# A fourth gate/up group in the space of late h tiles, q k v loads ahead of all groups, w_down loads late, and a p*v sum by a copied bank

## The chip, the cores and the metric

The kernel runs on one core of one Trainium2 chip. The metric is device time in microseconds (us) of one execution; lower is better. Times of profiled executions come from one execution each, and the median stands over three timed runs without a profile.

## The reference

One transformer-like block over 2048 tokens of width 576, in bf16. A layer norm feeds an attention with 32 heads of 18 columns and a sliding window of 256 tokens, and a gated feed-forward network of inner width 4608. The two results are multiplied and added to the input.

```python
xn = layernorm(x)                                   # 2048 x 576
q, k, v = split(xn @ wqkv)                          # 32 heads of 18
scores = q @ k.T * 18 ** -0.5, kept where 0 <= i - j < 256
s = (softmax(scores) @ v) @ wo
h = sigmoid(xn @ w_gate) * (xn @ w_up)              # 2048 x 4608
g = silu(h @ w_down)
out = x + s * g
```

## The kernel before

The tokens are worked in four chunks of 512 columns (`CH`, four blocks of 128). A chunk c passes these stages:

- **Layer norm** (`build_ln`): statistics and mean on VectorE, the power for the reciprocal deviation on POOL (`rstd`), normalising on VectorE (`apply`, L424), a copy of the first 64 columns behind the last (`wrap`, L428, so that two halves of TensorE's rows see matching pieces). In chunk 0 the result is transposed by TensorE (L447) and copied by ScalarE; in the others by a transposing DMA into `xn`.
- **Projections** (`build_qkv`, `project`, L468): twelve projections of 18 matmuls each. In chunk 0 q and k of a block go into one buffer (`pk` or a spare part of `expr`), and one transposing DMA per block brings both into `qkp`.
- **Attention**: `build_unit` computes scores (L613) into PSUM banks 0 to 3, ScalarE takes exponentials (L631), VectorE multiplies masks (L649). `build_pv` multiplies with v for a pair of head groups (L683), again into banks 0 to 3, two banks per head group, because the two halves of TensorE's rows fill a bank each. VectorE then transposes both banks of a head group (L699, L701), adds them (L704), divides (L713, L717) and transposes back (L723, `after_pv`); DMAs gather the heads in `oT`.
- **Gate and up** (`build_ffn`, L830): 36 tiles of 128 inner columns, 18 matmuls each. A tile's gate and up sums take two of the PSUM banks 4 to 7; ScalarE takes tanh (L844), VectorE forms the product (L848) and writes the tile into `hT`. The weights come in 12 groups of 3 tiles through a ring of `RW` = 3 buffers (`wgs`), each group by four DMAs (`load9`).
- **Down** (`f2`, L954, last block L984): four blocks of 128 tokens, each with 9 w_down loads' worth of matmuls (`op_wd`); the 9 loads happen once, in chunk 0, and stay. **wo** (`build_wo`, L760) multiplies the attention's result for two pairs of blocks. `build_final` forms the output (L1015 to L1023).

Between these stages the order isn't written by hand. Every piece of work is an `Op` with an engine, an estimated duration, dependencies and a priority; `schedule` is a greedy planner that places, at each step, the operation that can start first by these estimates, plus 40 ns per point of priority (`PRIO_NS`), and so fixes the instruction order of each engine. Dependencies in `odeps` and `behind` only order; those in `deps` also become semaphore waits (`emit`). All DMAs are issued by one queue, SP's, in the planner's order, so that one that waits holds up all behind it.

The first chunk differs from the others in that nothing is loaded yet. `QKV_LOAD` and `W_PRIO` set the order of the weights: q, v, group 0, k, groups 1 and 2, the transposes of q and k (L216), then group 3 and so on as ring buffers come free. `build_late_weights` lets w_down's load q go when gate/up tile 3 q + 8 is done.

Of the kernel before, what the change touches and what calls it, by code (L numbers as in the profile page):

```python
# [8 lines left out]
D = 576  # L9
# [25 lines left out]
RW = 3  # L35
RT = 2
# [17 lines left out]
WX_FT = 7  # L54
QKV_FIRST = "q0 q1 v0 v1 q2 v2 k0 v3 k1 q3 k2 k3"
# [3 lines left out]
QKV_CHAIN = 0  # L59
# [4 lines left out]
F2B = ((0, 1), (2, 3), (6, 7), (4, 5))  # L64
# [15 lines left out]
LN_STEP = 1  # L80
XT_CUT = 4
SC_GATE = 0
QKT_BEHIND = {2: 0}
# [3 lines left out]
QKV_LOAD = (-8, -4, -6)  # L87
W_PRIO = (-5, 2, 3)
# [4 lines left out]
XT0_BYTES = 1.2  # L93
# [83 lines left out]
class Builder:  # L177
# [46 lines left out]
    def alloc_memory(self):  # L224
# [44 lines left out]
        self.pkf = self.pk.bitcast(f32)  # L269

# [4 lines left out]
    def build(self):  # L275
# [22 lines left out]
        for c in range(NCH):  # L298
# [14 lines left out]
            if c == 0:  # L313
                self.build_late_weights()
                for o in self.ops:
                    if o.name.startswith("wo:0:") and o.fence is None:
                        o.add_dep(self.op_wo)

    def build_init(self):
# [22 lines left out]
        self.op_pkz = [op("ACT", 1300 + 1500, lambda e: e.memzero(self.pk[:, :, :, :]), "pkz", prio=0)]  # L342
        self.op_pkz.append(op("ACT", 2500, lambda e: e.memzero(self.expr[:, 0:3, :, :]), "pkz2", prio=0))
# [29 lines left out]
    def build_late_weights(self):  # L373
# [12 lines left out]
        for q in range(NWD):  # L386
            self.op_wd[q].add_dep(self.op_f1[(0, 3 * q + 8)])
# [7 lines left out]
    def build_ln(self, c):  # L395
# [4 lines left out]
        for i in range(QPC):  # L400
            st = c * QPC + i
            if c == 0:
# [15 lines left out]
            ve = op("DVE", 100, lambda e, st=st: e.tensor_scalar(self.veps[:, st, :], self.mv[:, st, 1:2], EPS,  # L418
                                                                None, ALU.add), f"ve:{st}", deps=[ag], prio=pr)
# [8 lines left out]
            wr = op("DVE", 100, lambda e, sr=sr: e.tensor_copy(self.xnr[:, sr, D:DP], self.xnr[:, sr, 0:64]),  # L428
                    f"wrap:{st}", deps=[ap], prio=pr)
# [10 lines left out]
            for i0, i1, dep in ((0, XT_CUT, ap), (XT_CUT, NC, wr)):  # L440
# [9 lines left out]
                tr = self.pe(n * 58, f_tr, f"tr:{st}", deps=[dep, self.op_ident] + dxn, prio=pr, psum=[ps])  # L450
# [8 lines left out]
        self.all_xn = [o for l in self.op_xn for o in l]  # L459

# [29 lines left out]
    def build_qkv(self, c):  # L490
# [4 lines left out]
        for w in order.split():  # L495
            i, j = int(w[1]), "qkv".index(w[0])
            o = (self.build_v if j == 2 else self.build_qk)(c, i, j, old)
            if c > 0:
                o.odeps += ([prev] if prev and QKV_CHAIN else []) + (self.op_xn[QKV_GATE] if not prev else []) + ([self.f2_ops[QKV_F2]] if QKV_F2 else [])
                o.prio = QKV_PRIO  # L500
            prev = o

    def build_qk(self, c, i, j, old):
# [8 lines left out]
        o, ps = self.project(c, i, j, f"qk:{c}:{i}:{j}", dpk, self.op_pv[c - 1][NHG - 1] if c > 0 else None)  # L512

        def f_ev(e):
# [5 lines left out]
            if j == 0:  # L520
# [3 lines left out]
                     deps=[o, self.op_pkz] + [t for t in (self.op_on[c - 1] if c > 0 else [])], prio=1, psum=[ps])  # L524
        if c == 0:
            if j == 0:
# [4 lines left out]
                          prio=0, issue=XT0_ISSUE_NS, transpose=True)  # L531
# [123 lines left out]
    def build_pv(self, c, a):  # L655
# [38 lines left out]
        bufs = {a: (self.tf[:, :, :, :].rearrange("p a b d -> p (a b d)"), pkf[1]), a + 1: (pkf[0], pkf[1])}  # L694
        ads = []
        qk = self.op_q + self.op_k
        for hg in pair:
            tf, tg = bufs[hg]
            t1 = self.rd("DVE", dve_ns(CH), lambda e, tf=tf, hg=hg: e.transpose(tf, self.bank(ps2[hg][0])),  # L699
                         f"t1:{c}:{hg}", deps=[o, self.last_mul] + qk, prio=3, psum=ps2[hg][:1])  # L700
            t3 = self.rd("DVE", dve_ns(CH), lambda e, tg=tg, hg=hg: e.transpose(tg, self.bank(ps2[hg][1])),  # L701
                         f"t3:{c}:{hg}", deps=[o, self.last_mul] + qk + ads, prio=3, psum=ps2[hg][1:])
            tf, tg = (t.rearrange("p (g d) -> p g d", d=32)[:, :, 0:DH + 1] for t in (tf, tg))
            ads = [self.op("DVE", dve_ns(16 * (DH + 1)), lambda e, tf=tf, tg=tg: e.tensor_tensor(tf, tf, tg, ALU.add),  # L704
                           f"ad:{c}:{hg}", deps=[t1, t3], prio=3)]
            bufs[hg] = (tf, ads[0])
        for hg in pair:
            self.after_pv(c, hg, o, *bufs[hg])

# [35 lines left out]
    def build_wo(self, c):  # L745
# [3 lines left out]
        for pair in ((0, 2), (1, 3)):  # L749
# [3 lines left out]
            def f_wo(e, swap, ps2=ps2, pair=pair):  # L753
                for kt in range(NKT - swap):
                    for n, (n0, n1) in enumerate(((0, 512), (512, D))):
                        for hf in range(2):
                            w = hf ^ swap
                            r0 = 64 * hf
                            qi = pair[w]
                            r = e.matmul(self.bank(ps2[w], n1 - n0, n), self.oT[r0:r0 + 64, kt, qi * P:(qi + 1) * P],  # L760
                                         self.wo_sb[r0:r0 + 64, kt, n0:n1], start=(swap == 0 and kt == 0),
                                         stop=(swap == 1 and kt == NKT - 2), tile_position=(r0, 0))
                return r
            wa = self.pe(NKT * (mm_ns(512) + mm_ns(64)), lambda e, f=f_wo: f(e, 0), f"wo:{c}:{pair[0]}",
                         deps=self.op_oc[c][0] + self.op_oc[c][1] + self.op_wo + [d for _, ds in slots for d in ds],
                         prio=WO_PRIO, psum=ps2, mode="r64")
            wo = self.pe((NKT - 1) * (mm_ns(512) + mm_ns(64)), lambda e, f=f_wo: f(e, 1), f"wo:{c}:{pair[0]}s",
                         deps=[wa], prio=WO_PRIO, mode="r64")
            wo.fence = wa
            for ps in ps2:  # L770
                ps.users.append(wo)
            for qi, ps, (ss, _) in zip(pair, ps2, slots):
                def f_se(e, ps=ps, ss=ss):
                    b = ps.banks[0] * 512
                    return e.activation(self.sat[:, ss, :], self.ps[:, b:b + D], ACTF.Copy, scale=0.25)
# [17 lines left out]
    def build_ffn(self, c):  # L793
        pg = [Psum((6,), (7,), (5,), (4,)) for _ in range(NFT)]
        pu = [Psum((6,), (7,), (5,), (4,)) for _ in range(NFT)]
        slots, dmas = {}, {}
# [20 lines left out]
        for n0, n1 in zip(cuts, cuts[1:]):  # L817
            if n1 - n0 > RUN:
                cuts.append(n0 + (n1 - n0 + 1) // 2)
# [4 lines left out]
        def step(e, half, gu, ft, i, x):  # L824
            r0 = 64 * half
            f0 = ft % FG * P
            w = (self.wgs[r0:r0 + 64, slots[ft // FG], i, f0:f0 + P] if x is None
# [441 lines left out]
```

## Time and profile before

| | us |
|---|---|
| median of three timed runs (566.16 to 566.95) | 566.52 |
| profiled execution, device time | 568.96 |
| its span, first to last instruction | 566.8 |
| TensorE busy in it | 558.1 |
| VectorE / ScalarE / POOL busy | 308.5 / 275.0 / 28.3 |

| stretch of the profiled execution | us |
|---|---|
| warm matmuls, transposes and eight projections | 1.52 to 17.49 |
| gate/up and the last four projections until the first scores | 17.49 to 37.55 |
| first chunk's down matmuls begin | 108.5 |
| down matmuls of chunks 1, 2, 3 begin | 246.9, 385.0, 523.1 |
| end | 566.8 |

The granted TensorE clock is 0.999 in the mean. Busy times are those of one execution; a row of the timeline gives start, duration, engine, line of the kernel, output and inputs, the number of instructions that follow each other, and in brackets the idle time before the first and what ended it. "PE" is TensorE, "DVE" VectorE, "ACT" ScalarE, "SPq" the queue that issues DMAs.

### The profile page before, as it was taken

The numbers are of one execution on the slowest core, as the hardware profiler recorded it, in microseconds if no ns is written. First come the engines' busy times: TensorE is split into PE (matmuls) and PEld (weight loads), VectorE is DVE, ScalarE is ACT, GpSimd is POOL, SyncE is SP. The second block draws the span as 40 slices with busy tenths as digits, with TensorE's granted clock in tenths as the row PEclk, the third lists the DMA queues.
The fourth block names the chain that finished last, engine by engine and source line by source line (L and its number), as shares of the span: only waits on it lengthen the run. The fifth ranks groups of instructions, "written<-read, shape, count | busy, mean of one in ns | idle before, by whom it ended". The sixth has DMA issues, their size and how long they took to land.

```text
span 566.8 us, 17897 instructions
## 1 busy us (share of the span) xinstructions
PE 558.1 (98%) x7854; PEld 282.9 (50%) x7854; DVE 308.5 (54%) x664; ACT 275.0 (49%) x372; POOL 28.3 (5%) x55
## 2 busy tenths in 40 slices
PE   8999989999999999999999999999999999999997
PEld 5644434457544444455654444545665444444544
DVE  6137987831236895782204778767120686686213
ACT  7447656403246847721406676581230856856011
POOL 3000100010000000010000011001000000000100
PEclk9999999999999999999999999999999999999999
DMA  8999999538966666324894665614669455650001
GB/s 198 212 200 232 237 216 219 131 71 104 164 128 148 149 138 148 87 47 77 110 213 103 143 154 130 152 46 61 98 111 210 97 127 128 147 130 23 20 22 43
DMA packets 125898, 73.29 MB, mean 129 GB/s; under 512 B 54654, under 2 KB 125310, under 8 KB 125822
## 3 DMA queue, kind: packets, MB, share of 16 engines
q1 hardware_dynamic: 125822, 72.16, 62.8%
q8 instruction: 62, 1.02, 0.8%
q14 instruction: 14, 0.11, 0.1%
HBM read 55.48 MB, written 2.36 MB: 102 GB/s over the span
## 4 chain that ended last, share of the span: by engine, by line
PE 94%; SPq 2%; DMA 2%; issue 1%; DVE 0%; ACT 0%
PE ps L830 50%; PE ps L954 23%; PE ps L468 8%; PE ps L613 5%; PE ps L683 4%; PE ps L760 3%; SPq L217 2%; PE ps L984 2%; DMA wqkv_sb<-in_A_wqkv_dram 1%; DMA qkp<-expr 1%; ACT expr L631 0%; DVE hT L848 0%; DVE expr L649 0%; DVE thf L1017 0%; ACT thf L1015 0%
## 5 line engine op out<-in xcount | busy, mean ns | idle before, releaser
L830 PE MATMUL ps<-xn,wgs 64*128 64x512 bf16 x2576 | 296.5, 377 | 0.2 <-DVE hT L848 0.2
L830 PEld LDWEIGHTS ps<-xn,wgs 64*128 64x128 bf16 x2576 | 119.5, 94 | 142.3 <-issue 7.6
L631 ACT ACTIVATE expr<-ps 128x1024 bf16<-128x1024 f32 x152 | 147.2, 1022 | 25.3 <-PE ps L613 25.3
L954 PE MATMUL ps<-wd_sb,hT 128*128 128x512 bf16 (+1 forms) x1080 | 133.7, 286 | 0.0
L844 ACT ACTIVATE tring<-ps 128x512 bf16<-128x512 f32 x144 | 86.3, 600 | 86.4 <-PE ps L830 84.4
L848 DVE SCALAR_TENSOR_TENSOR hT<-tring,ps 128x512 bf16<-128x512 bf16 x144 | 98.0, 680 | 31.5 <-ACT tring L844 15.0
L954 PEld LDWEIGHTS ps<-wd_sb,hT 128*128 128x128 bf16 x1080 | 68.3, 98 | 64.9 <-issue 1.4
L649 DVE TENSOR_TENSOR expr<-expr,m 128x512 bf16<-128x512 bf16 (+2 forms) x152 | 58.4, 412 | 53.7 <-ACT expr L631 52.5
L1015 ACT ACTIVATE thf<-ps 128x576 bf16<-128x576 f32 (+2 forms) x17 | 10.6, 623 | 134.3 <-PE ps L954 127.1
L1017 DVE SCALAR_TENSOR_TENSOR thf<-thf,ps 128x576 bf16<-128x576 bf16 (+2 forms) x17 | 12.2, 719 | 107.6 <-ACT thf L1015 107.6
L468 PE MATMUL ps<-wqkv_sb,xn 64*128 64x288 bf16 x864 | 54.7, 283 | 0.8 <-DMA wqkv_sb<-in_A_wqkv_dram 0.8
L468 PEld LDWEIGHTS ps<-wqkv_sb,xn 64*128 64x128 bf16 x864 | 42.5, 94 | 11.9 <-issue 2.0
L613 PE MATMUL ps<-qkp 18*64 18x320 bf16 (+4 forms) x1472 | 32.4, 259 | 0.9 <-DMA qkp<-expr 0.9
L613 PEld LDWEIGHTS ps<-qkp 18*64 18x64 bf16 x1472 | 16.2, 103 | 33.4 <-ACT expr L631 14.0
L660 POOL COPY qkp<-qkp 128x256 bf16<-128x256 bf16 x24 | 9.6, 401 | 282.2 <-PE ps L613 282.2
L683 PE MATMUL ps<-expr,vau 64*32 64x320 bf16 (+5 forms) x1440 | 20.9, 253 | 2.1 <-issue 1.9
L683 PEld LDWEIGHTS ps<-expr,vau 64*32 64x32 bf16 x1440 | 18.0, 92 | 9.6 <-issue 6.4
L723 DVE STREAM_TRANSPOSE op__63<-pk 128x512 bf16<-128x512 bf16 x32 | 22.3, 697 | 0.2
L521 DVE CAST pk<-ps 128x576 bf16<-128x576 f32 x13 | 9.8, 754 | 21.5 <-PE ps L468 21.5
L701 DVE STREAM_TRANSPOSE pk<-ps 128x512 f32<-128x512 f32 x32 | 21.5, 671 | 0.0
L760 PE MATMUL ps<-wo_sb,oT 64*128 64x512 bf16 (+1 forms) x288 | 18.7, 283 | 0.1
L699 DVE STREAM_TRANSPOSE tf<-ps 128x512 f32<-128x512 f32 x16 | 11.5, 717 | 13.0 <-PE ps L683 12.9
(54 smaller groups left out, 201.1 us busy)
## 6 DMA issues: line engine op xcount, KB each, us to landing
wgs<-in_B_w_gate_dram SPq DMA_DIRECT2D x48, 240.0 KB, 3.8
wgs<-in_B_w_up_dram SPq DMA_DIRECT2D x48, 240.0 KB, 4.8
wgs<-in_B_w_up_dram SPq DMA_DIRECT2D x48, 192.0 KB, 4.1
wgs<-in_B_w_gate_dram SPq DMA_DIRECT2D x48, 192.0 KB, 4.5
wd_sb<-in_B_w_down_dram SPq DMA_DIRECT2D x9, 576.0 KB, 7.7
xf<-in_A_x_dram SPq DMA_DIRECT2D x18, 144.0 KB, 2.3
out_dram<-xf SPq DMA_DIRECT2D x15, 144.0 KB, 2.0
xr<-in_A_x_dram SPq DMA_DIRECT2D x14, 144.0 KB, 5.0
```

The costliest lines, as they stand in the source:

```text
L468: r = e.matmul(self.bank(ps, HV, hf), self.xn[r0:r0 + 64, k, i * P:(i + 1) * P], self.wqkv_sb[r0:r0 + 64, j, k, :], start=(k == 0), stop=( ...
L613: r = e.matmul(self.ps[64 * half:64 * half + 64, b:b + n * 64], self.qkp[r0:r0 + DH, hg, k0:k0 + 64], self.qkp[r0:r0 + DH, hg, q0 * 64:(q0 ...
L631: return e.activation(self.expr[:, es, 2 * pr:2 * pr + 2, :], src, ACTF.Exp, scale=SM_SCALE)
L649: return e.tensor_tensor(ap, ap, m, ALU.mult)
L683: r = e.matmul(self.ps[32 * j:32 * j + 32, b + q0 * 64:b + (q0 + n) * 64], vf[:, v0:v0 + 32], self.expr[p0:p0 + 64, es, j, pos * 64:(pos + ...
L701: t3 = self.rd("DVE", dve_ns(CH), lambda e, tg=tg, hg=hg: e.transpose(tg, self.bank(ps2[hg][1])), f"t3:{c}:{hg}", deps=[o, self.last_mul] ...
L723: t2 = self.op("DVE", dve_ns(CH), lambda e, on=on: e.transpose(self.op_[:, hg % NOT, :], on.rearrange("p g d -> p (g d)")), f"t2:{c}:{hg}" ...
L760: r = e.matmul(self.bank(ps2[w], n1 - n0, n), self.oT[r0:r0 + 64, kt, qi * P:(qi + 1) * P], self.wo_sb[r0:r0 + 64, kt, n0:n1], start=(swap ...
L830: return e.matmul(self.bank((pg, pu)[gu][ft]), w, self.xn[r0:r0 + 64, i, :], start=first, stop=last, tile_position=(r0, 0))
L844: return e.activation(self.tring[:, st_, :], self.bank(ps), ACTF.Tanh, scale=0.5)
L848: return e.scalar_tensor_tensor(self.hT[:, ft, :], self.tring[:, st_, :], 1.0, self.bank(ps), ALU.add, ALU.mult)
L954: r = e.matmul(self.ps[:, b + n0:b + n1], lhsT, self.wd_sb[:, q, fl, n0:n1], start=(ft == 0), stop=(ft == NFT - 1))
```

## The change

The change has several parts, nearly all in the first chunk.

- **Loads.** The k weights come ahead of all groups. Group 3 of chunk 0 gets a place of its own: `far`, the space of `hT`'s tiles 29 to 35, which the products fill near the chunk's end. Its four loads stand ahead of the q/k transposes. A gate/up operation waits for the one of a group's four loads that it reads, no longer for all four.
- **w_down.** Load q waits for gate/up tile 14, 18, 22, 28, 29, 30, 31, 32, 33 and not for 8, 11, ..., 32.
- **Layer norm.** The addition of epsilon and the wrap go from VectorE to POOL; the wrap is computed from x and no longer copied from the normalised tile. Tiles' priorities are further apart.
- **Clearing.** ScalarE clears two buffers of `pk` and three parts of `expr` one by one, the last behind the transposes.
- **p*v in chunk 0** (`pv_by_copy`): ScalarE copies one bank of a head group into SBUF, VectorE adds the other bank to it and transposes the sum once.
- **wo** is cut into four passes of 288 columns (two per bank half), not two passes of 512 and 64. In chunks 1 to 3 the order of projections is fixed, and wo stands after the fourth and the sixth of them.
- **Priorities** of tanh, product and p*v change, a run of 9 steps is cut 4 + 5 and not 5 + 4, the last down block's banks have two candidates, and down matmuls after the first block come after the chunk's last p*v.

What the planner makes of it on TensorE in chunk 0, as matmuls in order (f gate/up, sc a unit of scores; a number per stretch):

```
before: 8 projections f10 4 projections f116 sc f28 sc f26 sc f18 sc f22 sc f24 pv f66 sc f24 sc f22 sc f22 sc f22 pv f42
        sc f22 sc f22 sc f22 sc f24 pv f40 sc f22 sc f22 sc f26 pv f6 down
after:  12 projections f188 sc f28 sc f22 sc f22 sc f24 sc f22 pv f26 sc f24 sc f22 sc f22 sc f22 pv f24
        sc f22 sc f22 sc f22 sc f24 pv f26 sc f22 sc f24 sc f32 pv f8 down
```

The diff, cut to its core:

```diff
+FAR = NFT - 7
+WD_AT = (14, 18, 22, 28, 29, 30, 31, 32, 33)
-QKV_CHAIN = 0
+QKV_CHAIN = 1
+QKV_WO = {"v1": (0,), "q2": (1,)}
-F2B = ((0, 1), (2, 3), (6, 7), (4, 5))
+F2B = ((0, 1), (2, 3))
-LN_STEP = 1
+LN_STEP = 3
+EZ = 2
+PV_PRIO = (2, 3)
+PC_PRIO = 1
+PV_COPY = (0,)
+TH_PRIO = 0
+HM_PRIO = -1
-QKT_BEHIND = {2: 0}
+QKT_BEHIND = {3: 0}
-QKV_LOAD = (-8, -4, -6)
-W_PRIO = (-5, 2, 3)
+QKV_LOAD = (-8, -6, -7)
+W_PRIO = (-5, -4, -3, -2)
...
+        self.far = self.hT[:, FAR:FAR + 7, :].rearrange("p t c -> p (t c)")[:, 0:NC * FG * P].rearrange(
+            "p (k c) -> p k c", k=NC)
...
-            self.op_wd[q].add_dep(self.op_f1[(0, 3 * q + 8)])
+            self.op_wd[q].add_dep(self.op_f1[(0, WD_AT[q])])
...
-            ve = op("DVE", 100, lambda e, st=st: e.tensor_scalar(self.veps[:, st, :], self.mv[:, st, 1:2], EPS,
+            ve = op("POOL", 100, lambda e, st=st: e.tensor_scalar(self.veps[:, st, :], self.mv[:, st, 1:2], EPS,
...
-            wr = op("DVE", 100, lambda e, sr=sr: e.tensor_copy(self.xnr[:, sr, D:DP], self.xnr[:, sr, 0:64]),
-                    f"wrap:{st}", deps=[ap], prio=pr)
+            wr = op("POOL", 200, lambda e, st=st, xs=xs, sr=sr: e.tensor_scalar(
+                self.xnr[:, sr, D:DP], xs[:, 0:64], self.mv[:, st, 0:1], self.rstd[:, st, :],
+                ALU.subtract, ALU.mult), f"wrap:{st}", deps=[rs, ag] + dr, prio=pr)
...
+    def pv_by_copy(self, c, pair, o, ps2, qk, tf, pk1, pk2):
+        before, adds = self.last_mul, []
+        for hg, t in zip(pair, (tf, pk1)):
+            cp = self.rd("ACT", act_ns(CH), lambda e, t=t, hg=hg: e.activation(t, self.bank(ps2[hg][1]), ACTF.Copy),
+                         f"pc:{c}:{hg}", deps=[o, before] + qk, prio=PC_PRIO, psum=ps2[hg][1:])
+            adds.append(self.rd("DVE", dve_ns(CH), lambda e, t=t, hg=hg: e.tensor_tensor(
+                t, self.bank(ps2[hg][0]), t, ALU.add), f"pa:{c}:{hg}", deps=[o, cp], prio=PV_PRIO[c > 0],
+                psum=ps2[hg][:1]))
+        tr = None
+        for hg, ad, t, u in zip(pair, adds, (tf, pk1), (pk2, tf)):
+            tr = self.op("DVE", dve_ns(CH), lambda e, t=t, u=u: e.transpose(u, t), f"pt:{c}:{hg}", deps=[ad, tr],
+                         prio=PV_PRIO[c > 0])
...
-                    for n, (n0, n1) in enumerate(((0, 512), (512, D))):
+            def f_wo(e, swap, n, ps2=ps2, pair=pair):
...
-                        sw, dw = self.r_w.take()
-                        slots[fg] = sw
-                        wp = W_PRIO[fg] if c == 0 and fg < RW else -2
+                        far = c == 0 and fg == RW
+                        sw, dw = (None, []) if far else self.r_w.take()
+                        slots[fg] = self.far if far else self.wgs[:, sw, :, :]
+                        wp = W_PRIO[fg] if c == 0 and fg <= RW else -2
...
-                        deps += dmas[fg]
+                        deps.append(dmas[fg][(half if i < 5 - half else 2 + half)])
...
+                                + ([self.op_pv[c][NHG - 1]] if q == 0 and i > 0 else []))
```

More of the change, by code (lines that the diff above doesn't have):

```diff
@@ L1189, in run_engine @@
                         continue
-                    if waits.get(k, -1) < v:
-                        waits[k] = v
-                for k, v in waits.items():
+                    if waits.get(k, (-1, 0))[0] < v:
+                        waits[k] = v, d.done
+                for k, (v, _) in sorted(waits.items(), key=lambda w: w[1][1]):
                     if known.get(k, -1) >= v:
```

97 lines of the change are left out of this document (59 added, 38 removed).

## The prediction

> **What bounds the kernel now.** I read the page's totals and its chain first, then TensorE's timeline from the start, because the chain hardly leaves TensorE.
>
> ```profile
> span 566.8 us, 17897 instructions
> PE 558.1 (98%) x7854; PEld 282.9 (50%) x7854; DVE 308.5 (54%) x664; ACT 275.0 (49%) x372; POOL 28.3 (5%) x55
> PE 94%; SPq 2%; DMA 2%; issue 1%; DVE 0%; ACT 0%
> ```
>
> TensorE is busy 558.1 of 566.8 us. The other 8.7 us are the most that any reordering can win, unless it also shortens TensorE's own instructions. The timeline of TensorE says where they lie ("idle before" stands in brackets):
>
> ```profile
> 1.52 4.45 PE L350 MATMUL ps<-hT 128*128 128x512 bf16 x10 [1.52 <-DVE neghalf L321]
> 6.00 1.23 PE L447 MATMUL ps<-op__63,xnr 128*128 128x128 bf16 x18
> ...
> 17.49 1.24 PE L830 MATMUL ps<-xn,wgs 64*128 64x512 bf16 x10
> 19.54 4.58 PE L468 MATMUL ps<-wqkv_sb,xn 64*128 64x288 bf16 x72 [0.81 <-DMA wqkv_sb<-in_A_wqkv_dram]
> 23.95 12.75 PE L830 MATMUL ps<-xn,wgs 64*128 64x512 bf16 x116
> 37.55 0.43 PE L613 MATMUL ps<-qkp 18*64 18x64 bf16 x24 [0.85 <-DMA qkp<-expr]
> ...
> 54.11 7.30 PE L830 MATMUL ps<-xn,wgs 64*128 64x512 bf16 x66
> ...
> 75.75 0.35 PE L683 MATMUL ps<-expr,vau 64*32 64x192 bf16 x17 [1.86 <-issue]
> ...
> 108.53 17.81 PE L954 MATMUL ps<-wd_sb,hT 128*128 128x512 bf16 x144
> ```
>
> Three gaps are inside the run: 0.81 us for the weights of k, 0.85 us for the transposed q and k, and 1.86 us in the middle of one p*v operation that has no wait in it ("issue"). The first two are what the new load order and the fourth group address. The third has no cause that this profile names. The profiled execution took 568.96 us (2.16 us outside its span), 2.44 us more than the median of 566.52; so I treat the 1.86 us as something that the timed runs may not have, and neither win nor lose it in the sum.
>
> **q, k, v loads ahead of all groups.** Today the four loads of group 0 stand ahead of k's. The chain and two windows of the DMA:
>
> ```profile
> 13.91 5.49 DMA wqkv_sb<-in_A_wqkv_dram
> 31.98 5.44 DMA qkp<-expr
> 15.00:20.00 5.00, 4.19 (x62) 2.81 (x60) 0.76 (x1) 1.34 (x3) 0.00 (x0) 1.00 1.17 218
> 20.00:25.00 5.00, 5.00 (x78) 4.11 (x76) 0.00 (x0) 2.61 (x4) 0.00 (x0) 1.00 1.14 217
> ```
>
> The last column is GB/s: the DMA is full and moves 218 per us in thousands of bytes. k lands at 19.40 (13.91 + 5.49). A group is 18 x 64 x 384 x 2 = 885 KB, so without it in front k lands 885 / 218 = 4.06 us earlier, at 15.3. In the new instruction order k0 is the seventh projection; today eight end at 17.49, and one takes 18 x 4.58 / 72 = 1.15 us, so it starts at 17.49 - 2.3 = 15.2. The 0.81 us go, and 0 to 0.3 us may come in their place. Group 0 then lands at 19.4 and is wanted after twelve projections, 17.49 + 4.58 = 22.1.
>
> **Fourth group, transposes of q and k later.** Group 3 has to go somewhere before its ring slot is free: into hT's last tiles, which are written near the end. Its four issues and the group's bytes now stand ahead of the transposes:
>
> ```profile
> 21.54 5.45 SPq L216 DMA_TRANSPOSE qkp<-pk  x1
> 27.09 8.16 SPq L216 DMA_TRANSPOSE qkp<-expr  x3
> 35.30 0.60 SPq L217 DMA_DIRECT2D wgs<-in_B_w_gate_dram  x1
> ```
>
> The first transpose's issue takes 5.45 us because loads are still queued in front of it. With 885 KB more, its end and all behind it move by 885 / 217 = 4.1 us: the last transpose lands at 37.42 + 4.1 = 41.5. TensorE now has 188 gate/up matmuls between the projections and the first scores (126 before), at 12.75 / 116 = 0.110 us each: 22.1 + 20.7 = 42.8. So the 0.85 us go, with 1.3 us to spare. Today the same 188 matmuls would be done at 37.55 + 62 x 0.110 = 44.4, so the two waits and their seams give 44.4 - 42.8 = **-1.6 us** at this point. The loads behind the transposes move too: group 4's issues start at 39.4; today group 3's last part, issued 2.0 us after its first, landed 4.8 us later:
>
> ```profile
> wgs<-in_B_w_up_dram SPq DMA_DIRECT2D x1, 240.0 KB, 4.8
> ```
>
> That makes 46.2 for group 4. It is wanted after scores, 28 matmuls and scores: 42.8 + 0.43 + 3.1 + 0.43 = 46.8. No cost, up to 0.5 us if late.
>
> **Layer norm, two small steps from VectorE to POOL.** The variance's epsilon and the 64 wrapped columns go to POOL; POOL runs epsilon, power, wrap for each tile in this order, one tile after the other. Today:
>
> ```profile
> 7.82 0.68 PE L447 MATMUL ps<-op__63,xnr 128*128 128x128 bf16 x9
> 3.39 0.44 DVE L413 BATCH_NORM_STATS2 bnst<-xr 128x6 f32<-128x288 bf16 x1
> 4.11 0.19 DVE L415 BATCH_NORM_AGGREGATE mv<-bnst 128x2 f32<-128x12 f32 x1
> 4.76 1.22 POOL L420 TENSOR_TENSOR rstd<-veps,neghalf 128x1 f32<-128x1 f32 x2 [1.83 <-DVE veps L418]
> 5.53 0.41 DVE L424 TENSOR_SCALAR xnr<-xr,mv,rstd 128x576 bf16<-128x576 bf16 x1
> 41.57 0.40 POOL L660 COPY qkp<-qkp 128x256 bf16<-128x256 bf16 x1 [32.82 <-PE ps L613]
> ```
>
> The statistics of tile 0 end at 3.83, and with the aggregate (0.19) and a handover POOL can start at about 4.2. A power takes 0.61. Wrap and epsilon aren't shown on POOL: the wrap lies between nothing and the 0.40 us of a copy four times as wide, I take 0.25; epsilon 0.1 to 0.2. So a tile needs about 1.0 to 1.2 us of POOL in series: the powers end at 5.0, 6.1, 7.3 and 8.5. Normalising takes 0.41 behind each. Tile 0 is ready well before TensorE ends its warm matmuls at 5.97, so nothing is won there; tile 1 is ready at about 6.7 to 7.0 (wanted at 6.6, halfway through the first 18 transposes), tile 2 at about 8.2 to 8.7 (wanted at 7.82), tile 3 in time. TensorE loses 0.5 to 1.0 us, **+0.6** taken (0 if POOL is as fast as VectorE on these).
>
> One pair of rows warns of more:
>
> ```profile
> 114.29 2.10 DVE L424 TENSOR_SCALAR xnr<-xr,mv,rstd 128x576 bf16<-128x576 bf16 x1
> 114.43 1.80 POOL L307 MEMSET pk<- 128x2048 bf16 x1 [10.14 <-DVE op__63 L723]
> ```
>
> The same normalising step took 2.10 us beside a POOL memset instead of 0.41: the two do not run side by side. The Trainium skill's page "SBUF — State Buffer", section "Who interferes with whom", says that GpSimd and a VectorE instruction in a two-port mode share a port pair as an exclusive lock, and the one that comes second waits for all of the other. The trace agrees in this pair. In the change, the wrap and the normalising of a tile are released by the same power. If they exclude each other, each tile's normalising starts a wrap later, 0.25 to 0.40 us: 0.5 to 0.8 us for tiles 1 and 2 on top. That is a rival below.
>
> **p*v sum by a copied bank (first chunk).** For a pair of head groups, four transposes and two adds on VectorE become two ScalarE copies, two adds out of PSUM and two transposes.
>
> ```profile
> L844 ACT ACTIVATE tring<-ps 128x512 bf16<-128x512 f32 x144 | 86.3, 600 | 86.4 <-PE ps L830 84.4
> L701 DVE STREAM_TRANSPOSE pk<-ps 128x512 f32<-128x512 f32 x32 | 21.5, 671 | 0.0
> L631 ACT ACTIVATE expr<-ps 128x1024 bf16<-128x1024 f32 x152 | 147.2, 1022 | 25.3 <-PE ps L613 25.3
> ```
>
> TensorE's work does not change. What changes is the cover: today 66, 42 and 40 gate/up matmuls stand between a p*v and the next scores, in the new order 26, 24 and 26, which is 2.6 to 2.9 us. The scores need all four banks back: two copies of 512 columns (0.60 each, as tanh) and the second add (0.67 as the nearest read of a bank by VectorE) make 1.87 us, and three handovers of at most 0.16 (power to normalising above: 4.76 + 0.61 to 5.53) 0.48: 2.35 us. It fits, **+0.1** taken for all three. At the upper end a copy costs a 1024-wide exponential's 1.02 and a tanh of 0.60 stands in front: 0.60 + 2.04 + 0.67 + 0.48 = 3.8 us, 1.1 us too long three times.
>
> **w_down mostly behind the last group.** Loads 3 to 8 are let go by matmul tiles 28 to 33 and not 17 to 32.
>
> ```profile
> wd_sb<-in_B_w_down_dram SPq DMA_DIRECT2D x9, 576.0 KB, 7.7
> 105.00:110.00 5.00, 4.98 (x106) 2.56 (x103) 3.48 (x7) 1.89 (x3) 0.00 (x0) 1.00 0.03 6
> ```
>
> The down matmuls start at some time T; load q is wanted at T + 2 q (17.81 us for nine). Tile 28 ends about 17 us before T. From the last group on, 0.9 MB of group, 0.7 MB of wo and six loads of 0.59 MB, 5.1 MB, need 23.5 us at 217: they end about at T + 2, load 8 being wanted at T + 16. They land where the DMA idles today (6 GB/s in that window). The transposes of xn behind them start some 2 us later. No cost; the cover is that 14 us.
>
> **wo in four passes, and its place.** 72 matmuls of mixed width took 4.59, and 288 wide ones 0.062 each (11.20 / 180), 4.48 for 72: no difference. In the last chunk wo is no longer cut in two by the down matmuls:
>
> ```profile
> 126.28 11.20 PE L468 MATMUL ps<-wqkv_sb,xn 64*128 64x288 bf16 x180
> 137.40 4.59 PE L760 MATMUL ps<-wo_sb,oT 64*128 64x512 bf16 x72
> 113.90 5.50 SPq L217 DMA_DIRECT2D oT<-op__63  x8
> 540.84 3.84 PE L760 MATMUL ps<-wo_sb,oT 64*128 64x512 bf16 x56
> 544.62 8.99 PE L954 MATMUL ps<-wd_sb,hT 128*128 128x512 bf16 x72
> 553.54 1.15 PE L760 MATMUL ps<-wo_sb,oT 64*128 64x512 bf16 x16
> ```
>
> 3.78 (540.84 to 544.62) and 1.09 (553.54 to the 554.63 of what follows, by its length) are 4.87, against 4.5 in one piece: **-0.4 us**. In the other chunks wo comes 6.6 us earlier, at T + 22; the last of its heads are issued by 119.40, T + 11, and even 2 us of w_down in front leave 9 us for their landing. The clearing of buffers on ScalarE, the order of x loads and the priorities of chunks 1 to 3 lie beside a TensorE that has no gap there; counted at nothing.
>
> **Sum.** -1.6 + 0.6 + 0.1 - 0.4 = -1.3 us: 567.7 for the profiled execution's 568.96 (with its 1.86 us left in), and 566.52 - 1.3 = **565.2** for the median. Its own range goes from 564.5 (layer norm at nothing) to 566.0 (1.0 there, 0.5 for a late group 4).
>
> **Rivals.** (1) The lock decides the start: +0.5 to +0.8 on top of the sum, 565.8; together with the range's upper end no change. For it: the 2.10 us row. Against: TensorE's first tile is covered by the warm matmuls.
>
> (2) The "issue" gap of 1.86 us is in the timed runs too and goes when the instructions around it move: 565.2 - 1.9 = 563.3. For it: it stands in a stretch with a full DMA. Against: the timed runs are 2.4 us shorter than the profiled one.
>
> (3) Slower: the scores after a p*v wait for ScalarE and VectorE. The change takes away 3 to 4 us of cover three times; at the 3.8 us chain it costs 3 x 1.1 = 3.3, 568.5. It makes the kernel slower than before by more than 0.2% only from 2.7 + 0.8 = 3.5 us of chain on. Against: the nearest rows are 512 wide at 0.60 and 0.67. For: in chunk 0 both engines also serve tanh and the product of every tile.
>
> (4) The change does not do what it says: the transposes land later than 42.8, because four more loads also slow their issue; each us is lost one for one. At the 8.16 us row stretched by a fifth, 1.6 us more, minus the 1.3 to spare: 565.5; with (1) 566.1.
>
> **How the numbers follow.** 0.2% is 1.13 us, about what a measurement of this kernel can tell from no change; the limits are 565.4 and 567.65. The forecast gets 0.50 (0.38 of it below 565.4), (2) 0.15, (1) and (4) together 0.18, within 0.2%, (3) 0.17. Faster 0.53, same 0.30, slower 0.17. The range has to take in (2) and the lesser half of (3): 563.2 to 567.6.
>
> **What would show it.** After: no gap ahead of the k projections, group 0's first matmuls straight behind twelve projections, first scores at 42 to 43.5 without a DMA wait, transposes done at about 41.5. The transposes of tiles 1 and 2 (second and third group of nine on TensorE) start 0.3 to 0.5 us late. Down matmuls of the first chunk start 1 us earlier, leaving the 1.86 us aside (about 107.5, or 105.6 without it). Chunk lengths behind that as now. The prediction is wrong if scores behind a p*v wait on VectorE or ScalarE, if a matmul waits for w_down or for group 4, or if the start loses more than 1 us.

## The result and the profile after

The changed kernel takes 565.79 us (median of 20 runs, 565.61 to 565.89); the kernel before, on the same chip, takes 567.58 us (20 runs, 566.16 to 570.29). The ratio is 0.9966, 95% interval 0.9957 to 0.9974: faster by 0.26 to 0.43%. Two things beside the medians matter for all that follows. The runs of the kernel before lie 4 us apart and those of the changed kernel 0.3 us. And the fastest runs of the two are only 0.55 us apart, so some 1.2 of the 1.8 us between the medians is that the long runs have gone. The profiled execution after took 565.84 us, 1.7 us more than its span.

The page of the changed kernel: totals, and the shares of the chain that ended last.

```profile
span 564.1 us, 17922 instructions
PE 555.5 (98%) x7831; PEld 287.7 (51%) x7854; DVE 302.9 (54%) x624; ACT 279.3 (50%) x382; POOL 44.0 (8%) x87
PE 96%; POOL 1%; issue 1%; DVE 1%; ACT 0%; DMA 0%; DVEq 0%; POOLq 0%
```

DMA had 2% of the chain and now has 0%; POOL was not in it and has 1%. TensorE's timeline says where each lies:

```profile
1.52 4.14 PE L363 MATMUL ps<-hT 128*128 128x512 bf16 x10 [1.52 <-DVE neghalf L333]
...
7.39 0.75 PE L462 MATMUL ps<-op__63,xnr 128*128 128x128 bf16 x9 [0.95 <-DVE xnr L437]
...
9.08 0.83 PE L462 MATMUL ps<-op__63,xnr 128*128 128x128 bf16 x9 [0.34 <-DVE xnr L437]
...
11.62 12.30 PE L486 MATMUL ps<-wqkv_sb,xn 64*128 64x288 bf16 x198
23.75 17.65 PE L874 MATMUL ps<-xn,wgs 64*128 64x512 bf16 x162
41.24 2.97 PE L874 MATMUL ps<-xn,hT 64*128 64x512 bf16 x26
44.13 0.43 PE L632 MATMUL ps<-qkp 18*64 18x64 bf16 x24
...
59.46 1.12 PE L702 MATMUL ps<-expr,vau 64*32 64x320 bf16 x72
60.51 2.98 PE L874 MATMUL ps<-xn,wgs 64*128 64x512 bf16 x26
63.42 0.42 PE L632 MATMUL ps<-qkp 18*64 18x320 bf16 x16
...
106.30 17.59 PE L1001 MATMUL ps<-wd_sb,hT 128*128 128x64 bf16 x141 [0.16 <-issue]
```

There is no gap ahead of the k projections and none ahead of the first scores. The scores behind p*v (59.46, 63.42) start without a wait. In the last row three matmul records of 144 are missing, and the 0.16 is their place, not a wait. New are the gaps ahead of the transposes of tiles 1 and 2. The chain of waits in the first 50 us shows what makes them (start, duration, piece):

```profile
4.20 0.25 POOL veps L431
4.45 0.07 issue
4.52 0.58 POOL rstd L433
5.10 0.10 issue
5.20 0.74 POOL xnr L441
5.94 0.21 POOL veps L431
6.15 0.07 issue
6.22 0.58 POOL rstd L433
6.80 0.10 issue
6.90 0.73 POOL xnr L441
```

Epsilon, power and wrap of a tile take POOL from 4.20 to 5.94 and the next from there: 1.70 us per tile, in series, on the path of the start. The queue of the DMAs has the transposes of q and k where they were forecast, and the issue of group 4 right behind:

```profile
24.44 6.35 SPq L226 DMA_TRANSPOSE qkp<-pk  x1
30.90 7.11 SPq L226 DMA_TRANSPOSE qkp<-expr  x3
38.06 0.73 SPq L227 DMA_DIRECT2D wgs<-in_B_w_gate_dram  x1
```

### The profile page after: what moved, and what is told of

It reads as the page before. It is cut to its first block, busy times and chain, and to the rows that moved or that the text cites. A ratio compares the mean times of both kernels' runs of the same rounds, so it can differ in the third digit from the quotient of the medians.

```text
span 564.1 us, 17922 instructions
## 1 busy us (share of the span) xinstructions
PE 555.5 (98%) x7831; PEld 287.7 (51%) x7854; DVE 302.9 (54%) x624; ACT 279.3 (50%) x382; POOL 44.0 (8%) x87
## 3 DMA queue, kind: packets, MB, share of 16 engines
q8 instruction: 62, 1.02, 0.8%
## 4 chain that ended last, share of the span: by engine, by line
PE 96%; POOL 1%; issue 1%; DVE 1%; ACT 0%; DMA 0%; DVEq 0%; POOLq 0%
PE ps L874 51%; PE ps L1001 23%; PE ps L486 9%; PE ps L632 5%; PE ps L702 3%; PE ps L795 3%; PE ps L1032 2%; POOL rstd L433 0%; POOL xnr L441 0%; DMA xr<-in_A_x_dram 0%; ACT expr L650 0%; POOL veps L431 0%; PE ps L462 0%; DVE hT L892 0%; DVE bnst L424 0%
## 5 line engine op out<-in xcount | busy, mean ns | idle before, releaser
L874 PE MATMUL ps<-xn,wgs 64*128 64x512 bf16 x2522 | 290.0, 377 | 0.2 <-DVE hT L892 0.2
L874 PEld LDWEIGHTS ps<-xn,wgs 64*128 64x128 bf16 x2522 | 116.4, 94 | 139.8 <-issue 10.3
L650 ACT ACTIVATE expr<-ps 128x1024 bf16<-128x1024 f32 x152 | 149.3, 1023 | 23.5 <-PE ps L632 23.5
L1001 PE MATMUL ps<-wd_sb,hT 128*128 128x64 bf16 (+1 forms) x1057 | 131.1, 284 | 2.1 <-issue 1.3
L1067 DVE TENSOR_TENSOR thf<-thf,sat 128x576 bf16<-128x576 bf16 (+2 forms) x17 | 7.5, 440 | 23.2 <-ACT sat L819 22.9
L795 PE MATMUL ps<-wo_sb,oT 64*128 64x288 bf16 x288 | 18.8, 283 | 0.2 <-issue 0.2
L319 POOL MEMSET pk<- 128x2048 bf16 x4 | 7.2, 1805 | 147.8 <-DVE op__63 L759 147.8
L541 ACT ACTIVATE pk<-ps 128x576 bf16<-128x576 f32 x13 | 8.5, 652 | 15.9 <-PE ps L486 13.6
```

Source lines behind the costliest of these rows:

```text
L650: return e.activation(self.expr[:, es, 2 * pr:2 * pr + 2, :], src, ACTF.Exp, scale=SM_SCALE)
L795: r = e.matmul(self.bank(ps2[w], HV, n), self.oT[r0:r0 + 64, kt, qi * P:(qi + 1) * P], self.wo_sb[r0:r0 + 64, kt, n * HV:(n + 1) * HV], st ...
L874: return e.matmul(self.bank((pg, pu)[gu][ft]), w, self.xn[r0:r0 + 64, i, :], start=first, stop=last, tile_position=(r0, 0))
L1001: r = e.matmul(self.ps[:, b + n0:b + n1], lhsT, self.wd_sb[:, q, fl, n0:n1], start=(ft == 0), stop=(ft == NFT - 1))
```

## The experiments

Three groups of four kernels, each together with runs of the kernel before: e1 to e4 on one chip, e5 to e12 on another. So e8 and e10 to e12 are compared with e1 and e2 across chips; e7, the changed kernel but for w_down's place, is the measure for e8 on its own chip. "Outside" is the time of a run less its span; "down" is where the first chunk's down matmuls start in the profiled execution, taken at their first record less the 0.16 where records are missing.

| kernel | median us | lowest to highest | runs | down | outside |
|---|---|---|---|---|---|
| before, beside e1 to e4 | 567.47 | 566.04 to 570.76 | 29 | | 2.2 |
| e1, the changed kernel | 565.65 | 565.61 to 565.88 | 11 | 106.04 | 1.75 |
| e2, changed, layer norm steps on VectorE | 564.71 | 564.45 to 565.49 | 7 | 104.36 | 2.2 |
| e3, the kernel before again | 567.20 | 565.99 to 570.68 | 8 | 105.73 | 2.2 |
| e4, before, w_down late | 567.01 | 566.06 to 567.58 | 12 | 105.65 | 2.2 |
| before, beside e5 to e8 | 567.24 | 566.14 to 572.11 | 35 | | |
| e5, before, k and v first | 567.33 | 566.54 to 569.13 | 12 | 106.28 | 2.2 |
| e6, before, k and v first, w_down late | 566.81 | 566.58 to 569.94 | 12 | 106.16 | 2.2 |
| e7, changed, w_down early | 565.71 | 565.55 to 566.61 | 12 | 106.01 | 1.75 |
| e8, changed, no fourth group | 566.36 | 566.17 to 566.97 | 12 | 106.18 | 1.7 |
| before, beside e9 to e12 | 567.05 | 566.37 to 571.13 | 28 | | |
| e9, before, layer norm steps on POOL | 567.09 | 566.64 to 571.56 | 12 | 107.04 | 1.75 |
| e10, changed, old p*v sum | 571.25 | 570.98 to 571.47 | 6 | | 1.75 |
| e11, changed, wrap alone on VectorE | 564.75 | 564.59 to 564.91 | 9 | 105.03 | 1.75 |
| e12, changed, layer norm on VectorE, no fourth group | 565.53 | 564.76 to 566.34 | 11 | 104.72 | 2.2 to 2.4 |

**e1 and e3: the two kernels once more.** No edit.

> The changed kernel once more, as the measure for the others on the same chip. Both theories: 565.6 to 565.9 us, a spread under 0.4 us, and in its profile the same three idle stretches of TensorE ahead of the transposes of tiles 1, 2 and 3 (0.95, 0.34 and 0.22 us).

> The kernel before, profiled a second time. Theory A (the kernel before loses time in its timed runs too, to gaps of TensorE that the trace calls issue, in the stretch where the DMA is full, 45 to 95 us; that is why its runs range from 566.2 to 570.3 and those of the changed kernel only from 565.6 to 565.9): one or more such gaps of over 1 us again, not necessarily at the same place, and the span longer by their sum than 564.7. Rival B (the gap of 1.86 us was an accident of one profile, and the spread comes from the two DMA waits at k and at the first scores): no gap over 0.5 us after 40 us, and the two waits together away from 1.66 us by over 0.5 us.

e1 repeats the result (ratio 0.9962, 0.9949 to 0.9976), e3 the kernel before (1.0006, 0.9982 to 1.0029). The profiled execution of e3 happened to be a short one (566.14), and its timeline shows what the long one of the prediction had besides:

```profile
23.47 12.75 PE L830 MATMUL ps<-xn,wgs 64*128 64x512 bf16 x116
36.76 0.43 PE L613 MATMUL ps<-qkp 18*64 18x64 bf16 x24 [0.54 <-DMA qkp<-expr]
```

The same program waits 0.54 us for the transposes and not at all for k, and the 1.86 us "issue" gap is not there. Its span, 563.9, is that of e1. TensorE also came later to the k projections: its first 18 transposes took 1.66 us and not 1.23, and the eight projections end 0.44 us later. So the waits that the change takes away are not one number: they vary from run to run, and on the best runs there is little to take.

**e2: the layer norm steps back on VectorE.**

```diff
-ve = op("POOL", 100, ... self.veps ... prio=0)
+ve = op("DVE", 100, ... self.veps ... prio=pr)
-wr = op("POOL", 200, ... e.tensor_scalar(self.xnr[:, sr, D:DP], xs[:, 0:64], ...), deps=[rs, ag] + dr, prio=pr)
+wr = op("DVE", 100, ... e.tensor_copy(self.xnr[:, sr, D:DP], self.xnr[:, sr, 0:64]), deps=[ap], prio=pr)
-LN_STEP = 3
+LN_STEP = 1
```

> The changed kernel with epsilon and wrap back on VectorE and the tile priorities of before; everything else, and TensorE's order from the projections on, as in the changed kernel. Theory A (POOL's serial chain of 1.7 us a tile is what cost the start 1.9 us): 1.5 to 1.9 us faster than the changed kernel, 563.8 to 564.3; the projections end at about 22.0 and not 23.9, the first scores come at about 42.2. Rival B (the start's delay is hidden, because the transposed q and k land only at about 41.3 and k at 15.3): less than 0.7 us faster, with a new wait of TensorE for a DMA at k0 or at the first scores of over 1 us.

0.94 us faster than e1 in the median, 0.9944 of the kernel before (0.9923 to 0.9964). TensorE's timeline:

```profile
6.09 1.17 PE L460 MATMUL ps<-op__63,xnr 128*128 128x128 bf16 x18 [0.39 <-DVE mv L428]
7.26 0.67 PE L484 MATMUL ps<-wqkv_sb,xn 64*128 64x288 bf16 x8
...
22.10 17.66 PE L872 MATMUL ps<-xn,wgs 64*128 64x512 bf16 x162
39.58 2.98 PE L872 MATMUL ps<-xn,hT 64*128 64x512 bf16 x26
42.50 0.43 PE L630 MATMUL ps<-qkp 18*64 18x64 bf16 x24
```

The gaps between the tiles are gone; gate/up starts at 22.10 and the first scores at 42.50, 1.6 us before the changed kernel's 44.13, and the down matmuls 1.68 us before e1's. That is what the two steps on POOL cost on TensorE. At the last block 1.53 of it are left; 0.45 are given back outside the span, and the rest of the difference to 0.94 is the wider spread of the runs.

**e4: w_down late, alone, in the kernel before.**

```diff
-self.op_wd[q].add_dep(self.op_f1[(0, 3 * q + 8)])
+self.op_wd[q].add_dep(self.op_f1[(0, (14, 18, 22, 28, 29, 30, 31, 32, 33)[q])])
```

> The kernel before with one part of the change alone: w_down's loads let go by tiles 14, 18, 22, 28 to 33. Theory A (w_down in the full stretch starves TensorE's instruction supply): the runs lose their spread, 566.2 to 566.8, about 1 us under the kernel before, and the profile has no issue gap over 0.5 us after 40 us. Rival B: the same as the kernel before within 0.3 us, same spread. In both the waits at k and the first scores stay, 0.8 us each.

Ratio 0.9986, 0.9972 to 1.0000. The median is 0.46 us lower, between the 1 us of theory A and the 0.3 of rival B, and the interval reaches 1. None of its 12 runs is over 567.6, which looked like a cause of the long runs; e6 and e7 test it. Its profiled execution (566.06) has neither the wait for k nor the one at the first scores, which both theories kept: no DMA wait of TensorE is in it at all.

**e5: k and v loaded first, alone, in the kernel before.**

```diff
-QKV_LOAD = (-8, -4, -6)
+QKV_LOAD = (-8, -6, -7)
```

> The kernel before with one constant changed: the loads of k and v go ahead of all gate/up groups, as in the changed kernel. Theory: two things of the start vary from run to run in the kernel before, the landing of k (0.81 us of waiting in the first profile, none in the second) and the landing of the transposed q and k (0.85 and 0.54), and a third, a stall of TensorE with no wait named (1.86 us in the first profile, none in the second), makes the long tail up to 570.8. Then this kernel loses only the first: no gap ahead of the k projections, lowest time unchanged (565.9 to 566.2), median 0.3 to 0.6 under the kernel before (about 567.0), highest still over 568.5. Rival: the whole spread is the start's transfers; then the median falls to about 566.3 and the tail goes.

Ratio 1.0002, 0.9985 to 1.0019: nothing gained in the median, and the lowest run rises by 0.4, which neither theory had. The timeline says why:

```profile
8.90 1.89 PE L468 MATMUL ps<-wqkv_sb,xn 64*128 64x288 bf16 x28 [0.39 <-DMA wqkv_sb<-in_A_wqkv_dram]
16.14 6.79 PE L468 MATMUL ps<-wqkv_sb,xn 64*128 64x288 bf16 x108 [0.22 <-DMA wqkv_sb<-in_A_wqkv_dram]
...
42.33 2.12 PE L830 MATMUL ps<-xn,wgs 64*128 64x512 bf16 x18 [0.78 <-DMA wgs<-in_B_w_up_dram]
```

The wait for k is down to 0.22 and the first scores don't wait, but TensorE waits 0.39 for earlier projection weights, and then the next transfer is late: group 3, whose loads stand behind the transposes. In this execution the load order alone moves the wait.

**e6: both, in the kernel before.** The edits of e4 and e5.

> The kernel before with k and v loaded ahead of all groups and with w_down's loads let go as late as in the changed kernel. Theory: the late w_down takes the stalls away (alone it brought the highest time from 570.8 to 567.6 and left the median at 567.0), the load order takes k's wait; what is left is the wait for the transposed q and k: median 566.2 to 566.7, highest under 567.4. Rival: the two do not add up, the transposes' landing makes the spread; then it stays at 567.0 like the late w_down alone.

566.81 (ratio 1.0001, 0.9982 to 1.0021), but three of 12 runs at 569.1 to 569.9: the late w_down does not take the long runs away, and e4's narrow range was chance or belongs to that order. The theory fell.

**e7: w_down early, in the changed kernel.** `WD_AT = (8, 11, 14, 17, 20, 23, 26, 29, 32)`.

> The changed kernel with w_down's loads let go as early as in the kernel before; TensorE's order is the same. Theory: TensorE's stalls come from the DMA being full between 40 and 110 us, so the spread comes back: lowest 565.6, median 566.0 to 567.0, highest over 567. Rival: the place of w_down is worth nothing, as the prediction counted it, and the narrow spread of the changed kernel comes from its start: 565.7, highest under 566.2.

565.71 beside e1's 565.65, 11 of 12 runs under 565.8 and one at 566.61, above the 566.2 that the rival allowed: the theory's spread does not come back, and no worth of w_down's place shows here.

**e8: no fourth group, in the changed kernel.**

```diff
-far = c == 0 and fg == RW
+far = False
-QKT_BEHIND = {3: 0}
+QKT_BEHIND = {2: 0}
-W_PRIO = (-5, -4, -3, -2)
+W_PRIO = (-5, -4, -3)
-wp = W_PRIO[fg] if c == 0 and fg <= RW else -2
+wp = W_PRIO[fg] if c == 0 and fg < RW else -2
```

> The changed kernel with the fourth gate/up group back in the ring of three, its loads behind the transposes of q and k; the load order of q, k, v and all the rest stay. 144 gate/up matmuls stand ahead of the first scores instead of 188. Theory: the layer norm steps already delay TensorE by 1.9 us, and with the transposes issued 4.1 us earlier again (landing at 37 to 38) the first scores at 23.9 + 144 x 0.110 = 39.7 find them landed; so the fourth group is worth nothing in the changed kernel: 565.4 to 565.9. Rival: the fourth group carries the gain of the start: first scores wait, 566.2 or more and a wide spread.

566.36, 0.7 over e1 and 0.65 over e7 on the same chip, so the theory that the fourth group is worth nothing beside the delay of the layer norm fell. But the rival's mechanism does not show either: in its profiled execution (566.31) the first scores start at 39.35 without a wait, and no DMA wait stands anywhere on TensorE. The down matmuls start 0.14 us later than e1's, the last block 0.29 us later, and 0.4 us more lie between the last VectorE instruction and the end of the span. What makes these differences stays open.

**e9: the layer norm steps on POOL, in the kernel before.** The changed kernel's lines L431 and L441, with its `LN_STEP` and the transposes' dependency on the normalising.

> The kernel before with the changed kernel's layer norm steps alone (epsilon and wrap on POOL). Theory: they hold TensorE back by 1.9 us ahead of the projections, and the waits for k and for the transposed q and k (0.5 to 1.7 us together, varying from run to run) vanish behind that; so it is not 1.9 but 0.3 to 1.3 us longer than the kernel before's best run on TensorE, and the spread shrinks: highest under 568. Rival: the long runs of the kernel before come from stalls that have nothing to do with the transfers of the start; then the median rises by 1 to 1.9 (568.2 to 569.2) and runs over 569 remain.

567.09 beside 567.05. The wait for the transposes is gone, as the theory has it, and again group 3 is what is late: 0.85 us.

```profile
43.05 2.12 PE L832 MATMUL ps<-xn,wgs 64*128 64x512 bf16 x18 [0.85 <-DMA wgs<-in_B_w_up_dram]
```

The lowest run is 0.27 us over that of the kernel before on this chip, the lower end of the theory. The rival's rise of the median did not come. But neither did the theory's end of the spread (highest under 568): one of the 12 runs took 571.56, 4.9 us over the lowest, more than all waits of the start seen in a profile (0.81 + 0.85).

**e10: the old p*v sum, in the changed kernel.** `PV_COPY = ()`.

> The changed kernel with the old sum behind p*v (four transposes and two adds on VectorE); the planner then puts 50, 44 and 36 gate/up matmuls behind each p*v instead of 26, 24 and 26, and the last scores and p*v of the first chunk fall behind the last gate/up matmul but eight, with nothing between scores and p*v. Theory: the copied bank is what lets the attention, started later behind the fourth group, still fit into the chunk; without it the last p*v waits for exponential and mask (about 2 to 3 us): 567 to 569. Rival: the sum by a copy is worth nothing, as the prediction's 0.1 has it: 565.6 to 566.0.

571.25, 5.6 us over e1 and outside the theory's range on the far side. The first chunk's last scores and p*v slip behind the last gate/up matmuls:

```profile
104.68 0.93 PE L1001 MATMUL ps<-wd_sb,hT 128*128 128x64 bf16 x7 [0.16 <-DVE expr L668]
106.18 0.42 PE L632 MATMUL ps<-qkp 18*64 18x320 bf16 x16 [0.58 <-ACT expr L650]
109.63 1.49 PE L702 MATMUL ps<-expr,vau 64*32 64x320 bf16 x72 [3.02 <-DVE expr L668]
111.45 17.68 PE L1001 MATMUL ps<-wd_sb,hT 128*128 128x64 bf16 x133 [0.34 <-issue]
```

0.58 + 3.02 = 3.6 us are waits for exponential and mask, where the theory had 2 to 3. (The two down rows hold 140 records of 144, and 0.16 and 0.34 can be the place of the missing ones.) The windows of the profile show what follows them; the last number but two is the granted clock:

```profile
106.00:108.00 2.00, 0.42 (x16) 0.16 (x16) 0.93 (x4) 1.45 (x3) 0.47 (x1) 1.00 0.78 155
108.00:110.00 2.00, 0.37 (x26) 0.40 (x33) 0.80 (x2) 0.62 (x1) 0.73 (x1) 1.00 0.43 86
110.00:112.00 2.00, 1.67 (x67) 1.30 (x52) 0.83 (x2) 0.00 (x0) 0.00 (x0) 0.55 0.32 74
112.00:114.00 2.00, 2.00 (x12) 0.87 (x11) 1.97 (x5) 0.00 (x0) 0.50 (x1) 0.59 0.00 0
114.00:116.00 2.00, 2.00 (x19) 1.05 (x18) 2.00 (x6) 0.00 (x0) 0.23 (x1) 1.00 0.40 80
```

TensorE was busy for 0.79 of the 4 us from 106 to 110, and for the next 4 us the granted clock was 0.55 and 0.59: by estimate 2 x 0.45 + 2 x 0.41 = 1.7 us lost. With the waits that is 5.3, and the first projection behind the down matmuls comes 5.24 us later than in the changed kernel (129.06, 123.82). The 1.86 us gap of the long execution before had no such sequel: its clock is 1.00 from 76 us on. This undoing also changes the planner's spacing (50, 44 and 36 matmuls behind a p*v), so it prices the copied bank together with the order that it allows.

**e11: the wrap alone back on VectorE.** The second pair of e2's lines; epsilon stays on POOL, `LN_STEP = 1`.

> The changed kernel with the wrap back on VectorE as a copy and epsilon left on POOL. Theory: the wrap's 0.74 us on POOL is most of the price; a tile then needs 0.24 + 0.57 and handovers, about 0.95 us of POOL instead of 1.75, and TensorE's projections start within 0.5 us of the kernel with all of it on VectorE: 564.2 to 565.0. Rival: epsilon and its handovers to and from POOL cost as much as the wrap: 565.2 to 565.7.

564.75, 0.9954 of the kernel before (0.9938 to 0.9969), range 0.3 us. POOL:

```profile
4.37 0.22 POOL L431 TENSOR_SCALAR veps<-mv 128x1 f32<-128x1 f32 x1 [1.46 <-DVE mv L428]
4.68 0.57 POOL L433 TENSOR_TENSOR rstd<-veps,neghalf 128x1 f32<-128x1 f32 x1
5.22 0.22 POOL L431 TENSOR_SCALAR veps<-mv 128x1 f32<-128x1 f32 x1
```

0.85 us per tile instead of 1.70, and on TensorE the only named wait left is the one at the very start. The down matmuls start 1.0 us before e1's and 0.7 after e2's: the wrap was the dearer of the two steps, epsilon the other 0.7. e11 and e2 are level (564.75, 564.71, on two chips), and both beat the changed kernel: e2 is 0.7 us earlier on TensorE, e11 takes 0.45 us less outside the span and has the narrower spread in its nine runs.

**e12: e2 and e8 together.**

> The changed kernel with the layer norm steps back on VectorE and without the fourth group in hT (its loads behind the transposes again). Theory: the fourth group pays where TensorE comes early: first scores are wanted at 22.1 + 15.7 = 37.8 and the transposes land at 37 to 38.5, so TensorE waits 0 to 0.8 us there, differently from run to run: median 565.0 to 565.9, spread over 1 us. Rival: with q, k, v ahead of all groups the transposes land in time without the fourth group too: 564.5 to 564.9, as with it.

565.53, range 1.6 us: the theory's numbers, 0.8 over e2. Its profiled execution (565.21) shows no wait ahead of the first scores at 38.01. Of the 0.36 us by which its down matmuls start after e2's, 0.28 are there when gate/up starts (22.38, 22.10), ahead of anything that the fourth group changes: its first 18 transposes take 1.70 us and e2's 1.17. So the theory's wait is not shown, and the place of the loss stays open. By the medians the fourth group is worth 0.7 to 0.8 us with and without the delay of the layer norm; by the lowest runs it is 0.6 (e8 against e7, one chip) and 0.3 (e12 against e2, two chips).

## Why the prediction was right, point by point

The forecast was 565.2 and the median is 565.79, faster by more than 0.2% as forecast. But three of the terms that make it up are not what the prediction had, and that the time came out so near is in good part luck. The forecast starts from 566.52, the median of three runs; the median of 20 is 567.58, from which the same -1.3 would have led to 566.3. Between the lowest runs the gain is only 0.55, and 0.45 of that lies outside the span, which the sum did not have: the spans of the short executions e3 and e1 are both 563.9, because the changed kernel is 0.3 us later at the first down matmuls (106.04, 105.73) and gets that back in wo. The other 1.2 us of the gain are the long runs, which stand in the prediction as rival (2) and not in the forecast.

- **The two DMA waits, -1.6: right in mechanism, and in size against that execution.** Both gaps are gone, the last transpose is issued at 38.01 (30.90 + 7.11) and the scores meet it landed. e2, which has this part without the layer norm's delay, starts its first scores at 42.50; the working said 42.8. What the step missed is that the waits vary: against e3 the same step is worth 105.73 - 104.36 = 1.4 us, and in e4's execution neither wait is there. And e5 shows that the order of the loads has no worth alone. The fourth group takes away the wait that would follow, for group 3; of group 4 the prediction had 0.5 us to spare, and no wait for it shows (its first matmuls, at 48.25, come 0.20 late for a product of VectorE).
- **Layer norm, +0.6: the failed step.** It is 1.6 to 1.7 us. The form was right (POOL in series, tiles 1 and 2 late); the term was mis-sized because the wrap was bounded by a copy of 256 columns, 0.40 us. A tensor_scalar with two scalars per partition takes 0.74 for 64 columns there (0.59 with no normalising step beside it), epsilon 0.24 where 0.1 to 0.2 was taken, and a tile 1.70 us where 1.0 to 1.2 was worked out. The bound came from another kind of operation, and a smaller tile did not make it an upper one. "If the start loses more than 1 us" was the prediction's own condition for being wrong, and it was met.
- **p*v copies, +0.1: no stall, 26 matmuls are enough.** But only the cost was asked for. e10 shows that without the copies the order breaks, at 5.6 us; the prediction did not see that the fourth group's later attention leans on them.
- **w_down, 0: right** (e7; e4's interval reaches 1). The idle windows behind the chunk fill as worked out, and no down matmul waits:

```profile
105.00:110.00 5.00, 4.84 (x62) 2.37 (x42) 4.01 (x9) 1.58 (x3) 0.00 (x0) 1.00 0.91 190
110.00:115.00 5.00, 4.95 (x42) 2.64 (x42) 3.91 (x5) 0.00 (x0) 3.01 (x3) 1.00 0.34 72
```

- **wo in one piece, -0.4: right in kind, -0.3 to -0.35 in size.** In the changed kernel wo takes 538.62 to 543.20 (the next row less its 0.16), 4.58 instead of 4.87, and e1 has 4.52.

```profile
538.62 4.58 PE L795 MATMUL ps<-wo_sb,oT 64*128 64x288 bf16 x72
543.36 8.77 PE L1001 MATMUL ps<-wd_sb,hT 128*128 128x64 bf16 x70 [0.16 <-issue]
```

- **Not in the sum: 0.45 us outside the span.** It fell from 2.2 to 1.75 and hid almost half of the layer norm's error: 565.2 + 1.05 (layer norm) - 0.1 (p*v) - 0.45 = 565.7, the waits and wo taken as forecast.

Of the rivals, (1), the lock, did not come as the prediction put it: no normalising step started a wrap later. It ran at once and in 0.43 us beside a wrap of 0.74, as long as with no wrap beside it (0.43 at 196.01). The third row is a wrap without a normalising step:

```profile
5.13 0.43 DVE L437 TENSOR_SCALAR xnr<-xr,mv,rstd 128x576 bf16<-128x576 bf16 x1
6.91 0.43 DVE L437 TENSOR_SCALAR xnr<-xr,mv,rstd 128x576 bf16<-128x576 bf16 x1 [0.63 <-POOL rstd L433]
65.67 0.59 POOL L441 TENSOR_SCALAR xnr<-xr,mv,rstd 128x64 bf16<-128x64 bf16 x1
```

By the exclusive lock of the Trainium skill's page "SBUF — State Buffer" ("Who interferes with whom") one of the pair would have waited for all of the other; wraps elsewhere in the changed kernel take 0.59 at least, so this pair would need about 0.43 + 0.59 = 1.02 us and needs 0.8. So the full lock shows beside the memset and not here. Some hindrance may be in the wrap all the same: the five that start within 0.1 us of a normalising step take 0.73 to 0.74, 0.15 more than the row above. And in the memset pair it was not the one that came second that waited: the normalising step had started first (114.29, the memset at 114.43) and ended last.

(2) was partly true: the kernel before has long runs in the timed executions too, and the changed kernel has none, which is why the median gains 1.8 us and the lowest run 0.55. In the kernels with the old p*v sum in the order of before (the kernel before and e3 to e6, e9) 21 of 168 runs lie over 568.5; of the 82 runs of the kernels with the copied bank none lies 2 us over its own lowest. e6 speaks against w_down's place as the cause alone, e7 too, and e9 against the layer norm. The longest of them have a mark: of the 11 runs of these kernels at 569.1 or more whose clock is on record, ten have a mean granted clock of 0.996 or 0.997, and no run under 569.1 has less than 0.999. e10's six runs all have 0.997, and there it goes with a gap of 3.02 us on TensorE. So a gap of that kind in the longest runs is likely; none of them was profiled, and it is not shown. Whether the long runs go with the copied bank, the other order of the gate/up matmuls or something beside them stays open: the one execution over 568.5 that was profiled has its 1.86 us inside a p*v.

(3) and (4) did not come: the scores behind p*v do not wait, and the last transpose lands at about 42.0 (35.7 + 6.3), 0.5 us after the forecast and ahead of the scores at 44.13.

## What to carry to other kernels

Price an operation that moves to another engine by that engine's row of the same kind, operands included; a wider operation of another kind is no upper bound, and a step on a serial start is paid in full by every tile. Profile the kernel before more than once before a wait is entered in a sum: here the waits of 0.81, 0.85 and 1.86 us of one execution were 0, 0.54 and 0 in another. And when a wait is taken away, ask which transfer comes next in the same queue (group 3 in e5 and e9). Of the parts tried alone in the kernel before, none gained anything clear of noise: neither the load order (e5), nor w_down (e4), nor both (e6); the copied bank and wo were not tried alone.

## What the runs showed of the hardware that was not expected

- POOL's price for small steps in the changed kernel's profile: 0.59 to 0.77 us for a tensor_scalar of 64 columns with two scalars per partition, 0.23 in the median for one column with a constant (up to 0.45 later in the run). In the kernel before VectorE copies the 64 columns in 0.18 us and adds the constant in 0.14.
- The time outside the span goes with the program: 1.7 to 1.8 us in all six kernels with epsilon on POOL (the changed one, e7 to e11), 2.15 to 2.4 in the six with it on VectorE. The pages of the first six list 15 or 16 packets on the second instruction queue, the others 14. That this is the cause was not shown.
- Behind 4 us in which TensorE was busy for 0.79 us, its granted clock stood at 0.55 to 0.59 for about 4 us (e10); behind a gap of 1.86 us it stayed at 1.00 (the kernel before).
- The first transposes on TensorE vary by themselves: in six of the 14 profiles (e3, e4, e7, e8, e11, e12) some of them take 311 to 314 ns, in the others 230 at most, with the granted clock at 1.00 in both.
